# A Strassen step in the first product of a mixture-of-experts layer, with token groups outermost, and a second buffer for z_prev

## The chip, the cores and the metric

The kernel runs on one core of one Trainium2 chip. The metric is the device time of one execution in microseconds (us). The engines have short names in what follows: PE is TensorE (PEld its weight loads), DVE is VectorE, ACT is ScalarE, POOL is GpSimd, and SP is the engine whose queue issues most DMA transfers. PE's results go to tiles in PSUM; the other tiles of the chip's own memory lie in SBUF.

## The reference, cut to what matters

```python
# attention with a memory, B=4, H=8, S=576, D=64
local   = softmax(causal(q @ k.T / sqrt(D))) @ v
q_p     = where(q > 0, q, exp(q) - 1) + 1
mem_out = (q_p @ M_prev) / (q_p . z_prev + 1e-6)
x       = sigmoid(beta) * mem_out + (1 - sigmoid(beta)) * local      # reshaped to [2304, 512]

# mixture of experts, N=2304 tokens, D=512, E=8 experts, F=1024
P = exp(x @ w_gate - max)
repeat 8 times:                      # Sinkhorn
    P /= P.sum(1) + 1e-9;  P /= P.sum(0) + 1e-9;  P *= N / E
out = sum over e of  P[:, e] * (max(x @ w1[e], 0) @ w2[e])
```

All inputs and the output are float32.

## The kernel before

The kernel has two stages that overlap a little. `attention()` works through 16 pairs of heads in a software pipeline. For each pair, `load` issues some twenty DMAs on SP's queue, among them three for `z_prev` into one tile `zb` (lines 227 to 236). `phi_` multiplies the feature map by `zb` on POOL (lines 270 and 274), `r_trans` sends a small table through DRAM and back on SP's queue (lines 447 to 456), and `comb` multiplies, splits and stores the result as two tiles `xh` and `xl` (lines 503 to 507). A value x is kept as a high part in the type float32r and a low part x - high; a product of two such values is three matmuls, high*high, high*low and low*high. In attention the order of PE's work is written out by hand (`tc.manual_schedule`, line 531); on the other engines, and for all engines in the experts, the Tile framework orders the instructions by the program's order and its own cost estimates, and puts in the semaphore waits.

`experts()` computes h = relu(x @ w1) and y = h @ w2. F is cut into quarters of 256 columns, so that there are 32 quarters over 8 experts. A quarter's first product (`layer1`, line 617) makes 2 row blocks of 128 for each chunk of tokens; a chunk is 512 tokens, four times, and 256 tokens, once. Each row block and chunk takes 4 blocks of the inner dimension times 3 passes, 12 matmuls. ACT takes relu out of PSUM into the high part (line 622) and DVE makes the low part from PSUM and the high part (line 623). The second product (`layer2`, line 636) makes a tile of 128 tokens by 512 columns with 6 matmuls per quarter, and DVE adds it to `acc`, scaled by the router's P (line 685). `acc` holds all 18 tiles of 128 tokens.

The order is weights outermost: a unit of work is a pair of quarters (`UNITS`, line 601), and within it all five chunks. So each quarter's weights are loaded once; `w_task` loads 256 KB on SP's queue into a ring of two buffers (`wst`) and POOL splits them (lines 117 and 118) while another unit is computed. Quarter 0 alone is computed for chunks 0 to 2 already inside attention, into a DRAM tile `ydr`, and read back into `acc` later (line 696). The router's eight Sinkhorn rounds (`rows` and `colsum`, lines 571 to 593) are strewn between the first units; each has eight small DVE instructions and one sum over partitions on PE (line 581). PSUM has six buffers for all of this (`ps_s`), plus one each with the tags x and f.

Of the kernel before, what the change touches and what calls it, by code (L numbers as in the profile page):

```python
# [17 lines left out]
def kernel(  # L18
# [13 lines left out]
    nc = tc.nc  # L32
# [24 lines left out]

    def w_slot(pool, nm):
        return {
            key: pool.tile([128, KD, FQ] if key[1] == "1" else [128, FQ // 128, DM], F32R,  # L60
                           name=f"{key}{nm}")
            for key in ("w1h", "w1l", "w2h", "w2l")
        }
# [5 lines left out]
    hq = [h_tiles(static, "0")]  # L69

    ident = const.tile([128, 128], F32, name="ident")
    hmask = const.tile([128, 2], F32, name="hmask")
    ident2 = const.tile([128, 64], F32, name="ident2")
    ones = const.tile([128, 128], F32, name="ones")
    mask = const.tile([128, 640], F32, name="mask")
    mask4 = const.tile([128, 288], F32, name="mask4")
    gcol = const.tile([128, HP, 9], F32, name="gcol")
    ogb = const.tile([128, HP, 2, 64], F32, name="ogb")
    gt = const.tile([128, 2, H], F32, name="gt")
# [5 lines left out]
    mx = const.tile([128, 2], F32, name="mx")  # L85

# [9 lines left out]
    def w_task(qu, j):  # L96
        e, part = divmod(qu, NQ)
        dst = slots[qu % len(slots)] if len(slots) > 1 else slots[0]
        raw = wst_p.tile([128, 512], F32, tag="wst", name="wst")
        if j < 2:  # L100
            nc.sync.dma_start(
                out=raw.rearrange("p (k f) -> p k f", k=2),
                in_=w1[e, 256 * j:256 * j + 256, part * FQ:part * FQ + FQ]
                .rearrange("(k p) f -> p k f", p=128),
            )
            hi, lo = (dst[a][:, 2 * j:2 * j + 2].rearrange("p k f -> p (k f)")
                      for a in ("w1h", "w1l"))
        else:
            r0 = part * FQ + (j - 2) * 128
            nc.sync.dma_start(out=raw, in_=w2[e, r0:r0 + 128, :])  # L110
            hi, lo = dst["w2h"][:, j - 2], dst["w2l"][:, j - 2]

        def split():
            if qu == 1:
                nc.scalar.copy(out=hi, in_=raw)  # L115
            else:
                nc.gpsimd.tensor_copy(out=hi, in_=raw)  # L117
            nc.gpsimd.tensor_tensor(out=lo, in0=raw, in1=f32(hi), op=ALU.subtract)  # L118

        return split  # L120


    def setup():
        make_identity(nc, ident)
        nc.vector.tensor_tensor(
            out=ident2, in0=ident[:, 0:64], in1=ident[:, 64:128], op=ALU.add
        )
        nc.vector.memset(ones, 1.0)
        nc.vector.memset(hmask, 0.0)
        for h in range(2):  # L130
            nc.vector.memset(hmask[64 * h:64 * h + 64, h:h + 1], 1.0)
# [49 lines left out]
    def attention():  # L181
        with ExitStack() as actx:
# [8 lines left out]
            zb = ap1.tile([128, 2, 128], F32, name="zb")  # L191
# [11 lines left out]
            for t_ in (*mraw, zb, qn4, e4t):  # L203
                nc.vector.memset(t_, 0.0)
# [4 lines left out]
            def load(p):  # L209
                b, hp = divmod(p, HP)  # L210
                for src, dst in ((q, qraw[p % 2]), (k, kraw[p % 2]), (v, vraw[p % 2])):
# [16 lines left out]
                    out=zb[:, 0, :],  # L228
# [3 lines left out]
                for h in range(2):  # L232
                    nc.sync.dma_start(
                        out=zb[half[h], 1, half[h]],
# [26 lines left out]
            def phi_(p):  # L261
                tmp = ap1.tile([128, 5, 128], F32, tag="tmp", name="tmp", bufs=1)
                phi = ap1.tile([128, 5, 128], F32, tag="phi", name="phi", bufs=2)
                st[p]["phi"], st[p]["tmp"] = phi, tmp
                nc.scalar.activation(out=tmp, in_=qraw[p % 2], func=AF.Exp)
# [256 lines left out]
            for j in range(4):  # L522
                seq.append((0.5 + 0.5 * j, lambda j=j: w_task(0, j)()))
# [77 lines left out]
    UNITS = [(0,), (1,)] + [(qu, qu + 1) for qu in range(2, E * NQ, 2)]  # L601
    NU = len(UNITS)
    LAST0 = NQ // 2

    def h_of(u, c, qu):
        return hq[(c if len(UNITS[u]) == 1 else qu) % len(hq)]

    def layer1(u, c, m, ps_new):
        c0, cn = CHUNKS[c]
        qu = UNITS[u][m // 2]  # L610
        ws, (hh, hl) = slots[qu % len(slots)], h_of(u, c, qu)
        f = m % 2
        pt = ps_new()
        n = 0
        for kt in range(KD):
            for wt, x in ((ws["w1h"], xh), (ws["w1h"], xl), (ws["w1l"], xh)):
                nc.tensor.matmul(  # L617
                    out=pt[:, 0:cn], lhsT=wt[:, kt, 128 * f:128 * f + 128],
                    rhs=x[:, kt, c0:c0 + cn], start=(n == 0), stop=(n == 3 * KD - 1),
                )  # L620
                n += 1
        nc.scalar.activation(out=hh[:, f, 0:cn], in_=pt[:, 0:cn], func=AF.Relu)  # L622
        nc.vector.scalar_tensor_tensor(  # L623
            out=hl[:, f, 0:cn], in0=pt[:, 0:cn], scalar=0.0, in1=f32(hh[:, f, 0:cn]),
            op0=ALU.max, op1=ALU.subtract,
        )

    def layer2(u, c, j, ps_new):
        pt = ps_new()
        cols = slice(128 * j, 128 * j + 128)  # L630
        n, last = 0, 6 * len(UNITS[u]) - 1
        for qu in UNITS[u]:
            ws, (hh, hl) = slots[qu % len(slots)], h_of(u, c, qu)
            for f in range(2):
                for h_, wt in ((hh, "w2h"), (hh, "w2l"), (hl, "w2h")):
                    nc.tensor.matmul(  # L636
                        out=pt, lhsT=h_[:, f, cols], rhs=ws[wt][:, f],
                        start=(n == 0), stop=(n == last),
                    )
                    n += 1  # L640
        return pt

# [4 lines left out]
    ydr = dram.tile([NEARLY * 4, 128, DM], F32, name="ydr")  # L647

    def early_parts():
# [3 lines left out]
        def l2(c, j):  # L653
            pt = layer2(0, c, j, ps_f)
            yst = wst_p.tile([128, DM], F32, tag="wst", name="wst")
            nc.vector.tensor_copy(out=yst, in_=pt)
            nc.sync.dma_start(out=ydr[4 * c + j], in_=yst)

        parts = []
        for c in range(NEARLY):  # L660
            parts.append(
                [lambda c=c, m=m: layer1(0, c, m, ps_f) for m in range(2)]
                + [lambda c=c, j=j: l2(c, j) for j in range(4)]
            )
        return parts

    def experts():
        mp = ctx.enter_context(tc.tile_pool(name="mp", bufs=1, reuse_waits="tile"))
        slots.extend(w_slot(mp, str(j)) for j in (1, 2, 3))
        hq.append(h_tiles(mp, "1"))  # L670
        acc = mp.tile([128, NTILE, DM], F32, name="acc")

# [3 lines left out]
        def part2(u, c, j):  # L676
            pt = layer2(u, c, j, ps_t)
            e = UNITS[u][0] // NQ
            t_ = CHUNKS[c][0] // 128 + j
            if u == 0:  # L680
                nc.vector.tensor_copy(out=acc[:, t_], in_=pt)
            elif e == 0:
                nc.vector.tensor_tensor(out=acc[:, t_], in0=pt, in1=acc[:, t_], op=ALU.add)  # L683
            else:
                nc.vector.scalar_tensor_tensor(  # L685
                    out=acc[:, t_], in0=pt, scalar=P[:, t_, e:e + 1], in1=acc[:, t_],
                    op0=ALU.mult, op1=ALU.add,
                )
            if u == NU - 1:
                eng = nc.sync if t_ % 2 == 0 else nc.scalar  # L690
                eng.dma_start(out=out[128 * t_:128 * t_ + 128, :], in_=acc[:, t_])

        for j in range(4):
            w_task(1, j)()
        for t_ in range(4 * NEARLY):
            nc.sync.dma_start(out=acc[:, t_], in_=ydr[t_])
        for u in range(NU):
# [59 lines left out]
```

## Time and profile before

| what | value |
|---|---|
| median of 3 runs | 1880.23 us (1879.83 to 1882.64) |
| the profiled execution | 1881.86 us, span in its profile 1880.1 us |
| granted TensorE clock, mean | 0.985 |
| PE / PEld busy | 96% / 80% of the span |
| DVE / ACT / POOL busy | 35% / 20% / 20% of the span |
| DMA | 67.12 MB, mean 36 GB/s |

A view of groups gives one line for all instructions of one source line, engine, operation and shape: how many, their busy time in us, the mean duration of one in ns, and the idle time of the engine just before them with what ended it. Matmuls are pipelined and the profile models their ends, so that the rows of matmuls in a stream overlap; what one costs in a stream is the distance from its start to the next one's start. A view of stretches gives each engine's busy time and number of instructions in a stretch of the span. The chain of waits is followed back from the last instruction, at each step to what released it; a piece of the chain with a count, over several instructions in a row, is the time that these took together.

### The profile page before, as it was taken

To read this page: it belongs to the slowest core of one execution; us is meant where nothing else is said; L and a number is where in the kernel's file an instruction comes from. 1 tells how busy PE (TensorE), PEld (TensorE's weight loads), DVE (VectorE), ACT (ScalarE), POOL (GpSimd) and SP (SyncE) were. 2 spreads that over 40 slices of the span, in tenths; PEclk is the share of its full clock that TensorE was granted. 3 is DMA by queue.
4 is the path that set the end of the run, shared out by engine and by line. 5 is a ranking of instruction groups with operands and counts; after the bars stand their busy time and mean duration, and the time that the engine had idled before them with its cause. 6 is when DMAs were issued, how large, how long until landed. Compare 5 with 4: busy or idle time off the path is not lost.

```text
span 1880.1 us, 22876 instructions
## 1 busy us (share of the span) xinstructions
PE 1808.5 (96%) x9147; PEld 1496.3 (80%) x9147; DVE 660.4 (35%) x1423; ACT 367.0 (20%) x877; POOL 369.4 (20%) x423
## 2 busy tenths in 40 slices
PE   5788888899999999999999999999999999999999
PEld 4566676788888888888888888888888888888887
DVE  6767674733322222222222222222222222222222
ACT  4666565011111111011111111111111111111110
POOL 4544444410303020111202030303030303030000
PEclk8989899999999999999999999999999999999999
DMA  4333323200101010000101010101010101010011
GB/s 105 97 80 87 84 53 126 82 23 1 46 0 40 6 30 16 21 25 12 34 6 40 1 46 1 45 1 45 0 46 1 46 0 46 1 34 1 1 45 56
DMA packets 101546, 67.12 MB, mean 36 GB/s; under 512 B 67264, under 2 KB 85824, under 8 KB 101440
## 3 DMA queue, kind: packets, MB, share of 16 engines
q1 hardware_dynamic: 100144, 63.30, 11.9%
q10 hardware_dynamic: 1296, 2.36, 0.3%
q8 instruction: 72, 1.18, 0.3%
q14 instruction: 34, 0.28, 0.0%
HBM read 57.69 MB, written 7.94 MB: 35 GB/s over the span
## 4 chain that ended last, share of the span: by engine, by line
PE 86%; DMA 3%; DVE 3%; POOL 3%; ACT 2%; issue 2%; SPq 1%; ACTq 0%; POOLq 0%; DVEq 0%
PE s L617 41%; PE s L636 40%; ACT e L333 1%; DMA wst<-in_moe_w_dram 1%; DMA rsb<-rd 1%; PE x L479 1%; PE s L370 1%; DVE e L326 1%; PE f L636 1%; PE s L312 1%; POOL xc L503 1%; ACT e L356 1%; DMA zb<-in_z_prev_dram 1%; POOL tmp L270 0%; POOL phi L434 0%
## 5 line engine op out<-in xcount | busy, mean ns | idle before, releaser
L617 PE MATMUL s<-xh,w1h 128*128 128x512 f32 (+1 forms) x1256 | 463.0, 369 | 0.0
L617 PE MATMUL s<-xl,w1h 128*128 128x512 f32 (+1 forms) x1256 | 462.4, 368 | 0.0
L617 PE MATMUL s<-xh,w1l 128*128 128x512 f32 (+1 forms) x1256 | 462.3, 368 | 0.0
L622 ACT ACTIVATE hh<-s 128x512 fp32r<-128x512 f32 (+1 forms) x314 | 174.0, 554 | 1366.8 <-PE s L617 1327.8
L636 PE MATMUL s<-w2h,hh 128*128 128x512 f32 x1128 | 439.7, 390 | 0.0
L636 PE MATMUL s<-w2h,hl 128*128 128x512 f32 x1128 | 438.8, 389 | 0.4 <-DVE hl L623 0.4
L636 PE MATMUL s<-w2l,hh 128*128 128x512 f32 x1128 | 438.8, 389 | 0.0
L623 DVE SCALAR_TENSOR_TENSOR hl<-s,hh 128x512 fp32r<-128x512 f32 (+1 forms) x314 | 199.9, 637 | 600.9 <-ACT hh L622 600.8
L685 DVE SCALAR_TENSOR_TENSOR acc<-s,P,acc 128x512 f32<-128x512 f32 x252 | 189.2, 751 | 463.2 <-PE s L636 463.2
L617 PEld LDWEIGHTS s<-xl,w1h 128*128 128x128 f32 x1256 | 237.4, 189 | 39.7
L617 PEld LDWEIGHTS s<-xh,w1h 128*128 128x128 f32 x1256 | 237.3, 189 | 39.6
L617 PEld LDWEIGHTS s<-xh,w1l 128*128 128x128 f32 x1256 | 237.3, 189 | 39.3
L117 POOL CAST w1h<-wst 128x512 fp32r<-128x512 f32 x62 | 38.0, 612 | 1073.5 <-PE s L617 1055.8
L636 PEld LDWEIGHTS s<-w2h,hl 128*128 128x128 f32 x1128 | 211.6, 188 | 45.5 <-DVE hl L623 1.6
L636 PEld LDWEIGHTS s<-w2h,hh 128*128 128x128 f32 x1128 | 211.8, 188 | 44.1 <-ACT hh L622 1.0
L636 PEld LDWEIGHTS s<-w2l,hh 128*128 128x128 f32 x1128 | 211.8, 188 | 42.9
L118 POOL TENSOR_TENSOR w2l<-wst,w2h 128x512 fp32r<-128x512 f32 x64 | 82.4, 1289 | 8.1 <-ACT w2h L115 3.1
L118 POOL TENSOR_TENSOR w1l<-wst,w1h 128x512 fp32r<-128x512 f32 x64 | 82.9, 1295 | 5.3 <-ACT w1h L115 0.5
L333 ACT ACTIVATE e<-e,mn 128x512 f32<-128x512 f32 (+3 forms) x128 | 70.3, 550 | 21.0 <-DVE mn L326 21.0
L326 DVE CUSTOM_DVE_ANT_0 e<-s,mask 128x512 f32<-128x512 f32 (+3 forms) x128 | 55.1, 484 | 9.0 <-PE s L312 9.0
L117 POOL CAST w2h<-wst 128x512 fp32r<-128x512 f32 x62 | 37.9, 611 | 58.1 <-PE s L636 42.1
L683 DVE TENSOR_TENSOR acc<-s,acc 128x512 f32<-128x512 f32 x36 | 24.9, 691 | 33.0 <-PE s L636 32.9
(169 smaller groups left out, 1129.2 us busy)
## 6 DMA issues: line engine op xcount, KB each, us to landing
wst<-in_moe_w_dram SPq DMA_DIRECT2D x128, 256.0 KB
rsb<-rd SPq DMA_DIRECT2D x32, 144.0 KB
qraw<-in_q_dram SPq DMA_DIRECT2D x32, 128.0 KB
kraw<-in_k_dram SPq DMA_DIRECT2D x32, 128.0 KB
vraw<-in_v_dram SPq DMA_DIRECT2D x32, 128.0 KB
ydr<-wst SPq DMA_DIRECT2D x12, 256.0 KB
acc<-ydr SPq DMA_DIRECT2D x12, 256.0 KB
out_dram<-acc SPq DMA_DIRECT2D x9, 256.0 KB
```

Source lines behind the costliest of these rows:

```text
L117: nc.gpsimd.tensor_copy(out=hi, in_=raw)
L118: nc.gpsimd.tensor_tensor(out=lo, in0=raw, in1=f32(hi), op=ALU.subtract)
L312: nc.tensor.matmul(out=sp[h][:, at:at + w], lhsT=qq[x][half[h], 128 * i:128 * i + 128], rhs=kk[y][half[h], 0:w], start=(a == 0), stop=(a = ...
L326: nc.vector.tensor_tensor_reduce(out=et[:, h, 0:w], in0=sp[h][:, at:at + w], in1=mask[:, c0:c0 + w], scale=-SCALE, scalar=3.0e38, op0=ALU. ...
L333: nc.scalar.activation(out=et[:, h, 0:w], in_=et[:, h, 0:w], func=AF.Exp, scale=-1.0, bias=mn[:, c:c + 1], accum_out=sm_[:, c:c + 1],)
L356: nc.scalar.activation(out=e4[:, 0:576], in_=e4[:, 0:576], func=AF.Exp, scale=-1.0, bias=mn[:, 8:9], accum_out=sm_[:, 8:9],)
L617: nc.tensor.matmul(out=pt[:, 0:cn], lhsT=wt[:, kt, 128 * f:128 * f + 128], rhs=x[:, kt, c0:c0 + cn], start=(n == 0), stop=(n == 3 * KD - 1),)
L622: nc.scalar.activation(out=hh[:, f, 0:cn], in_=pt[:, 0:cn], func=AF.Relu)
L623: nc.vector.scalar_tensor_tensor(out=hl[:, f, 0:cn], in0=pt[:, 0:cn], scalar=0.0, in1=f32(hh[:, f, 0:cn]), op0=ALU.max, op1=ALU.subtract,)
L636: nc.tensor.matmul(out=pt, lhsT=h_[:, f, cols], rhs=ws[wt][:, f], start=(n == 0), stop=(n == last),)
L683: nc.vector.tensor_tensor(out=acc[:, t_], in0=pt, in1=acc[:, t_], op=ALU.add)
L685: nc.vector.scalar_tensor_tensor(out=acc[:, t_], in0=pt, scalar=P[:, t_, e:e + 1], in1=acc[:, t_], op0=ALU.mult, op1=ALU.add,)
```

## The change

The first product is done in seven half-size products in place of eight. Tokens are cut into three groups of 768 (`NG`, two halves of `HT` = 384 tokens), the inner dimension into two halves of 256, and the quarter into its two row blocks of 128. With weights A (blocks a11, a21, a12, a22) and tokens B, the weights' combinations are made for every item by POOL, with ACT taking their high parts (`w1_split`); the four combinations of tokens are made once per group (`t_tasks`). Seven products of 6 matmuls of 384 tokens each go to three PSUM buffers (`prod`); ACT copies the first, DVE adds the others up in SBUF tiles X, U2 and U3 (`temps`), and the four results are taken through relu and split from SBUF (`relu_split`). The second product (`second`) is as before, on items of one quarter each, so 6 matmuls to a PSUM tile and one DVE addition to `acc`.

The order is now groups outermost: for each group, all quarters but the first, which is done for all tokens beforehand through `ydr`. So there are 93 items, and each item loads and splits its weights anew. The first two items and the two before each change of group use the plain product (`plain`): 4 results of 12 matmuls of 384 tokens. In an item, the products of item q are interleaved with the six tiles of the second product of item q-1, and pieces of the weights' split (`jobs`), of the router (`tick`) and of the next group's combinations (`todo`) are strewn between them. `acc` holds one group, is written out with the group's last item, and read again from `ydr`.

In attention, `zb` becomes two tiles in turn. The tiles used only by attention, and those used only by quarter 0, move to pools that are closed after use; two tiles that nothing reads are dropped.

```diff
-            zb = ap1.tile([128, 2, 128], F32, name="zb")
+            zb2 = [ap1.tile([128, 2, 128], F32, name=f"zb{j}") for j in range(2)]
...
-        mp = ctx.enter_context(tc.tile_pool(name="mp", bufs=1, reuse_waits="tile"))
-        slots.extend(w_slot(mp, str(j)) for j in (1, 2, 3))
...
+    HT = 384
+    NG = NT // (2 * HT)
...
+        ITEMS = [
+            (g, e, part) for g in range(NG) for e in range(E) for part in range(NQ)
+            if (e, part) != (0, 0)
+        ]
+        per = E * NQ - 1
+        plain = {0, 1} | {g * per - j for g in range(1, NG) for j in (1, 2)}
...
+        def t_tasks(g):
+            th, tl = tcomb
+            s0, s1, s2 = (temps[:, i] for i in range(3))
+            d, p_ = nc.vector, nc.gpsimd
...
+            def split(i, src, eng):
+                nc.scalar.copy(out=th[:, i], in_=src)
+                sub(tl[:, i], src, f32(th[:, i]), eng)
+
+            return [
+                lambda: full(s0, 0, 1, d), lambda: full(s1, 0, 0, d), lambda: full(s2, 1, 1, p_),
+                lambda: sub(s1, s0, s1, d), lambda: split(0, s1, p_), lambda: sub(s0, s2, s0, d),
+                lambda: split(2, s0, p_), lambda: sub(s2, s2, s1, d), lambda: full(s0, 1, 0, d),
+                lambda: split(1, s2, p_), lambda: sub(s0, s0, s2, d), lambda: split(3, s0, d),
+            ]
...
+            raws = [mp.tile([128, 512], F32, tag="raw", name="raw", bufs=2) for _ in range(2)]
...
+            def comb_a():
+                tt(out=a22, in0=a21, in1=a22, op=ALU.add)
+                tt(out=a21, in0=a11, in1=a21, op=ALU.subtract)
+
+            def comb_b():
+                tt(out=a11, in0=a22, in1=a11, op=ALU.subtract)
+                tt(out=a12, in0=a12, in1=a11, op=ALU.subtract)
+
+            if q in plain:
+                return [lambda: two(1, r1), lambda: one(0, a11), lambda: one(3, a21)]
+            return [
+                lambda: two(1, r1), lambda: one(0, a11), comb_a, comb_b,
+                lambda: two(3, r0), lambda: two(5, r1),
+            ]
...
+        def relu_split(q, f, th, src):
+            hh, hl = hs[q % 2]
+            c = slice(HT * th, HT * th + HT)
+            nc.scalar.activation(out=hh[:, f, c], in_=src, func=AF.Relu)
+            nc.vector.scalar_tensor_tensor(
+                out=hl[:, f, c], in0=src, scalar=0.0, in1=f32(hh[:, f, c]),
+                op0=ALU.max, op1=ALU.subtract,
+            )
+
+        def prod(q, ops):
+            pt = pp[count[0] % 3]
+            count[0] += 1
+            wh, wl = w1s[q % 2]
+            n, total = 0, 6 * len(ops)
+            for wi, (xh_, xl_) in ops:
+                for k in range(2):
+                    for w, x in ((wh, xh_), (wh, xl_), (wl, xh_)):
+                        nc.tensor.matmul(
+                            out=pt[:, 0:HT], lhsT=w[:, wi, k], rhs=x[:, k],
+                            start=(n == 0), stop=(n == total - 1),
+                        )
+                        n += 1
+            return pt[:, 0:HT]
...
+            def p1():
+                nc.scalar.copy(out=X, in_=prod(q, [(0, b11)]))
+            def p6():
+                add(U2, prod(q, [(3, t2)]), X)
+            def p2():
+                add(X, prod(q, [(1, b21)]), X)
+                relu_split(q, 0, 0, X)
+            def p7():
+                add(U3, prod(q, [(4, t3)]), U2)
+            def p4():
+                add(X, prod(q, [(2, t4)]), U3)
+                relu_split(q, 1, 0, X)
+            def p5():
+                pt = prod(q, [(6, t1)])
+                add(U2, pt, U2)
+                add(U3, pt, U3)
+                relu_split(q, 1, 1, U3)
+            def p3():
+                add(U2, prod(q, [(5, b22)]), U2)
+                relu_split(q, 0, 1, U2)
+            return [[p1, p6, p2], [p7, p4], [p5, p3]]
...
+        jobs = w1_split(0, w1_load(0))
+        acc_load(0)
+        for c in range(NEARLY, len(CHUNKS)):
+            for f in first_parts(c, ps_s):
+                f()
+                if c == NEARLY:
+                    tick()
+                if jobs:
+                    jobs.pop(0)()
...
+        for q in range(NI + 1):
+            jobs = []
+            if q < NI:
+                jobs += w2_split(q, r2.pop(q))
+            if q + 1 < NI:
+                jobs += w1_split(q + 1, w1_load(q + 1))
+                jobs.insert(2, lambda q=q: r2.__setitem__(q + 1, w2_load(q + 1)))
+            if q in plain and q + 1 in plain and q:
+                todo += t_tasks(q // per + 1)
+            groups = (first_plain if q in plain else first_fast)(q) if q < NI else [[], [], []]
+            for i, grp in enumerate(groups):
...
+                if q:
+                    for j in (2 * i, 2 * i + 1):
+                        second(q - 1, j)
...
+            if q < NI and q and q % per == 0:
+                acc_load(q // per)
```

More of the change, by code (lines that the diff above doesn't have):

```diff
@@ L108, in w_task @@
         else:
-            r0 = part * FQ + (j - 2) * 128
-            nc.sync.dma_start(out=raw, in_=w2[e, r0:r0 + 128, :])
+            r0 = (j - 2) * 128
+            nc.sync.dma_start(out=raw, in_=w2[0, r0:r0 + 128, :])
             hi, lo = dst["w2h"][:, j - 2], dst["w2l"][:, j - 2]
[L113 to L120, printed above, removed]
+        nc.gpsimd.tensor_copy(out=hi, in_=raw)
+        nc.gpsimd.tensor_tensor(out=lo, in0=raw, in1=f32(hi), op=ALU.subtract)
     def setup():
         make_identity(nc, ident)
-        nc.vector.tensor_tensor(
-            out=ident2, in0=ident[:, 0:64], in1=ident[:, 64:128], op=ALU.add
-        )
         nc.vector.memset(ones, 1.0)
-        nc.vector.memset(hmask, 0.0)
-        for h in range(2):
-            nc.vector.memset(hmask[64 * h:64 * h + 64, h:h + 1], 1.0)
         nc.gpsimd.memset(mask, 0.0)
@@ new lines, in w1_split, with one, two @@
+        def w1_split(q, raws):
+            wh, wl = w1s[q % 2]
+            r0, r1 = (r.rearrange("p (k f c) -> p k f c", k=2, f=2) for r in raws)
+            a11, a21, a12, a22 = r0[:, :, 0], r0[:, :, 1], r1[:, :, 0], r1[:, :, 1]
+            tt = nc.gpsimd.tensor_tensor
+            def one(i, src):
+                nc.scalar.copy(out=wh[:, i], in_=src)
+                tt(out=wl[:, i], in0=src, in1=f32(wh[:, i]), op=ALU.subtract)
+            def two(i, raw):
+                src = raw.rearrange("p k f c -> p f k c")
+                nc.scalar.copy(out=wh[:, i:i + 2], in_=src)
+                tt(out=wl[:, i:i + 2], in0=src, in1=f32(wh[:, i:i + 2]), op=ALU.subtract)
+            def comb_a():
[9 more added lines that the diff above has]
+                lambda: two(3, r0), lambda: two(5, r1),
+            ]
@@ new lines, in w2_split, with one @@
+        def w2_split(q, raws):
+            wh, wl = w2s[(q + 1) % 2]
+            def one(j):
+                nc.scalar.copy(out=wh[:, j], in_=raws[j])
+                nc.gpsimd.tensor_tensor(
+                    out=wl[:, j], in0=raws[j], in1=f32(wh[:, j]), op=ALU.subtract
+                )
+            return [lambda: one(0), lambda: one(1)]
+        def relu_split(q, f, th, src):
[5 more added lines that the diff above has]
+                op0=ALU.max, op1=ALU.subtract,
+            )
@@ new lines, in second, with acc_load @@
+            if q % per == per - 1:
+                eng = nc.scalar if g == NG - 1 and j % 2 else nc.sync
+                eng.dma_start(out=out[128 * t_:128 * t_ + 128, :], in_=acc[:, j])
+        def acc_load(g):
+            for j in range(2 * HT // 128):
+                nc.sync.dma_start(out=acc[:, j], in_=ydr[2 * HT // 128 * g + j])
+        NI = len(ITEMS)
+        jobs = w1_split(0, w1_load(0))
[7 more added lines that the diff above has]
+                    jobs.pop(0)()
```

245 lines of the change are left out of this document (142 added, 103 removed).

## The prediction

> **What bounds the kernel now.** I read the page first, then the stretches, then the end of the chain of waits.
>
> ```profile
> span 1880.1 us, 22876 instructions
> PE 1808.5 (96%) x9147; PEld 1496.3 (80%) x9147; DVE 660.4 (35%) x1423; ACT 367.0 (20%) x877; POOL 369.4 (20%) x423
> ...
> PEclk8989899999999999999999999999999999999999
> ```
>
> In the stretches the columns after the length are each engine's busy time (number of instructions), the granted clock, the DMA share and GB/s.
>
> ```profile
> 300.00:350.00 50.00, 40.33 (x220) 30.97 (x218) 20.92 (x62) 13.63 (x35) 25.08 (x29) 0.93 0.46 143
> 900.00:1100.00 200.00, 200.00 (x929) 167.59 (x928) 53.58 (x78) 22.81 (x41) 32.65 (x36) 1.00 0.08 24
> ```
>
> From about 360 us on PE is never idle and runs at the full clock, as in the second stretch; DVE, ACT and POOL are busy 27%, 11% and 16% of it. The experts' time is therefore the number of matmuls times the distance between their starts. The end of the chain gives that distance, since its pieces are runs of matmuls with nothing between them (start, length, what):
>
> ```profile
> 1843.15 10.88 PE s L617 x48
> 1854.03 10.88 PE s L636 x48
> 1864.91 5.75 PE s L617 x48
> ...
> 1876.17 0.75 DVE acc L685
> ```
>
> A matmul with 512 tokens costs 10.88/48 = 0.2267 us in both products; one with 256 tokens (the short chunk) 5.75/48 = 0.1198. So an instruction costs nearly what its width says, and the weight load of each one hides at least down to 0.12 us.
>
> **First product: the gain.** No expert matmul is 384 wide. A line through the two widths gives 0.1198 + (0.2267 - 0.1198)/2 = 0.1733 us; strict proportion to 512 gives 0.170. I take 0.1733, as it lies on both rows. The first quarter stays; 31 are left.
> - Before, a quarter takes 4 chunks x 24 x 0.2267 + 24 x 0.1198 = 24.64 us; 31 take 763.8.
> - After, 87 fast items take 7 x 6 = 42 matmuls, 7.28 us each, 633.2; 6 plain items take 48, 8.32 us each, 49.9; together 683.1.
> - Gain 80.7 us (93.8 at 0.170).
>
> The second product keeps its count: 93 items x 6 tiles x 6 = 3348, as 31 quarters x 18 tiles x 6. An item's share is 36 x 0.2267 = 8.16 us, so a fast item has a **PE period of 15.44 us**.
>
> The Trainium skill, "TensorE: Matmul & The Clock Gate", section "Back-to-back issue gap", puts an isolated warm matmul at N/2.4 + 2.5 ns. That would be 0.216 us at 512 and 0.1625 at 384; the trace has 0.2267 at 512, so the rule is too low here; by it alone the fast items would save another 87 x 42 x 0.0108 = 39 us.
>
> **What must fit behind those 15.44 us.** The new work runs on engines that were idle, so I cost it by the nearest shapes.
>
> ```profile
> L685 DVE SCALAR_TENSOR_TENSOR acc<-s,P,acc 128x512 f32<-128x512 f32 x252 | 189.2, 751 | 463.2 <-PE s L636 463.2
> L623 DVE SCALAR_TENSOR_TENSOR hl<-s,hh 128x512 fp32r<-128x512 f32 x250 | 172.8, 691 | 537.0 <-ACT hh L622 536.9
> L623 DVE SCALAR_TENSOR_TENSOR hl<-s,hh 128x256 fp32r<-128x256 f32 x64 | 27.0, 423 | 63.9 <-ACT hh L622 63.9
> L267 DVE SCALAR_TENSOR_TENSOR phi<-qraw,tmp 128x640 f32<-128x640 f32 x16 | 14.0, 874 | 0.4 <-issue 0.2
> L622 ACT ACTIVATE hh<-s 128x512 fp32r<-128x512 f32 x250 | 149.5, 598 | 1131.7 <-PE s L617 1092.6 <-DMA out_dram<-acc 39.1
> L622 ACT ACTIVATE hh<-s 128x256 fp32r<-128x256 f32 x64 | 24.5, 383 | 235.1 <-PE s L617 235.1
> L118 POOL TENSOR_TENSOR w1l<-wst,w1h 128x512 fp32r<-128x512 f32 x64 | 82.9, 1295 | 5.3 <-ACT w1h L115 0.5
> L507 POOL TENSOR_TENSOR xl<-xc,xh 128x256 fp32r<-128x256 f32 x16 | 11.7, 732 | 1.3 <-ACT xh L506 1.3
> ```
>
> - DVE, per fast item: 7 additions out of PSUM at 384, half way between 691 and 423 = 0.557, 3.9 us; 6 additions to acc at 0.751, 4.5; 4 low parts from SBUF, 0.55 (874 x 384/640, 0.52, and a little for the fixed part), 2.2. Sum 10.6. Each low part first waits for ACT's relu, about 0.49 (between 598 and 383): up to 2.0 more, if nothing fills it.
> - ACT: a copy and 4 relus at 0.49, 2.5; weights' high parts, five at 0.6 and one at 0.38, 3.4. Sum 5.9.
> - POOL: w2, 2 x 1.29; w1, 3 x 1.29 + 5 x 0.73 (four combinations, one low part). Sum 10.1.
>
> All below 15.44, so covered. What is queued behind what: ACT's high parts stand in its queue behind the relus, and these behind PE's products; DVE's acc additions stand behind low parts that wait for ACT. Three buffers for products and three for tiles give PE some 3 us before a late addition stops it: p6 reuses the buffer of p5, read by 13.0 us of the item, at 15.44 + 1.04.
>
> A second bound is DVE's waiting for POOL. Rows in order of time (start, length):
>
> ```profile
> 343.14 1.27 POOL L118 TENSOR_TENSOR w1l<-wst,w1h 128x512 fp32r<-128x512 f32 x1
> ...
> 343.63 0.94 DVE L575 TENSOR_TENSOR Pt<-P,rs 128x144 f32<-128x144 f32 x1
> ...
> 363.82 0.31 DVE L575 TENSOR_TENSOR Pt<-P,rs 128x144 f32<-128x144 f32 x1
> ```
>
> The same DVE instruction, both inputs in SBUF, takes 0.31 alone and 0.94 when it starts inside a POOL instruction: it ends 0.16 us after POOL's. The low parts out of PSUM do not show it (mean 691 beside a POOL 16% busy). In the new item the 4 low parts have both inputs in SBUF, and POOL is busy 10.1 of 15.44 us, so each waits between 0 and 1.29 us; I take 65% x half of 1.1 = 0.36, 1.4 per item. DVE then needs 10.6 + 1.4 + 2.0 = 14.0 of 15.44 us.
>
> The Trainium skill, "SBUF — State Buffer", section "Who interferes with whom", says the same as a rule: a DVE instruction with two SBUF inputs contends with a GpSimd instruction that reads SBUF, and whichever is second blocks fully. This rule speaks against the change; the trace agrees (0.94 against 0.31).
>
> **The weights' cycle.** Raw w1 has two buffers and an item needs both, so the next load starts when POOL has finished this item's split.
>
> ```profile
> 337.72 2.66 DMA wst<-in_moe_w_dram
> ```
>
> A load lands 2.66 us after the wait before it ends. Then ACT 0.6, POOL 7.5, one more wait for ACT 0.6: 11.4 us, and 13 with hand-offs and with POOL blocked by DVE (up to 4 x 0.55). The 2.6 us for w2 fit into the load's wait. Below 15.44, so covered, and the last two combinations are needed only at p5, 10.6 us into the next item. For small stalls in a fast item I take 0.1 us (bounds 0 and 0.3), +8.7 for 87.
>
> **Start of the experts.** PE's stalls there now (the bracket is the idle time before):
>
> ```profile
> 325.30 0.61 PE L550 MATMUL s<-ident,ls 16*128 16x16 f32 x4 [5.08 <-ACT ls L546]
> ...
> 326.43 0.63 PE L617 MATMUL s<-xl,w1h 128*128 128x512 f32 x1
> 326.86 0.63 PE L617 MATMUL s<-xh,w1l 128*128 128x512 f32 x1
> ...
> 355.61 0.48 PE L581 MATMUL cp<-Pt,ones 128*128 128x144 f32 x2 [1.95 <-DVE Pt L575]
> ```
>
> The 5.08 us wait for a buffer of the ring that the weight loads share; w1's raw tiles now have their own. Matmuls after it start 0.43 apart, twice the usual, 12 of them: 2.4 us more. Up to 12 us can go, with the router's waits. New is DVE's load in items 0 and 1: seven of eight router rounds (2.2 us each, from the round below less its wait), 8 combinations of 768 columns (874 x 768/640 = 1.05 each), 8 low parts at 0.557 and 6 additions at 0.69: 15.4 + 8.4 + 4.5 + 4.1 = 32 us, before waits for POOL, against PE's 2 x 8.32 + 8.16 = 24.8.
>
> ```profile
> 362.99 0.29 DVE L572 TENSOR_REDUCE rs<-P 128x18 f32<-128x144 f32 x1
> ...
> 364.80 0.31 DVE L585 TENSOR_REDUCE cs<-cp 128x8 f32<-128x144 f32 x1 [0.67 <-PE cp L581]
> ...
> 365.59 0.31 DVE L590 SCALAR_TENSOR_TENSOR P<-Pt,cs 128x144 f32<-128x144 f32 x1
> ```
>
> So PE idles 7 us there, or 18 with waits for POOL; less what goes, -5 to +11. I take +3 (bounds -12 and +11).
>
> **Changes of group, attention, tail.** SP issues nine loads of acc in a row now:
>
> ```profile
> 320.67 4.31 SPq L696 DMA_DIRECT2D acc<-ydr  x9
> ```
>
> At each change it has 6 stores and 6 such loads to issue (0.48 us each); the last acc load waits for the last store, 2.66 or so, and the next weights' load stands behind it, about 5 us late. The cycle has 2.4 us of slack per item, and the late combinations are needed late: +2 each, two of them (bounds 0 and 10 each), +4. The next combinations of tokens, 12 tasks, fall into two plain items, where DVE has only 4 x 0.557 + 4.5 = 6.7 of 16.5 us to do, so nothing; without that cover they cost DVE's 8 us. In attention, SP waits for POOL to free zb:
>
> ```profile
> SPq L227 <- POOL tmp L270: 2.9, 3, 1.5
> SPq L227 <- POOL tmp L274: 1.9, 5, 0.5
> ```
>
> That is 4.8 us in 8 waits, with the r table's load queued behind some; the two waits go, the load of the first pair doesn't move. What is late next is that table. I take -2 (bounds -5 and +2, as the order on SP is made anew). Dropped and moved tiles: nothing, they stand ahead of the first loads. The last item's six stores come 1.36 us apart instead of 2.72: +1 (0 to 2).
>
> **Sum.** -80.7 + 8.7 + 3 + 4 - 2 + 1 = -66.0. From the profiled execution, 1881.9 (span 1880.1), that is 1815.9; it lies 1.6 above the median of the runs, 1880.23, so I forecast **1814 us**. Its own range, from the bounds: 1797 to 1842.
>
> **Rivals.**
> - *DVE becomes the bound, through its waits for POOL (slower).* If the four waits are 1.0 us each, DVE needs 10.6 + 2.0 + 4.0 = 16.6 us per fast item, 1.2 over PE: 87 x 1.2 = 104, less the 8.7 counted, 1909. It decides from a period of 15.44 + (66 + 8.7)/87 = 16.3 us on. For it: the 0.94 row. Against: POOL isn't always busy, and acc additions can fill the waits for relu.
> - *The weights' cycle or ACT's queue sets the period, partly.* 13 us with 2.4 us of slack; if ACT's high parts come 3 us late behind relus, the period is about 16.0: 87 x 0.56 - 8.7 = +40, 1854. For it: one load's buffers in effect; against: late weights are needed late.
> - *The narrow matmul is cheaper or the start clean.* 0.170 and no new stall at the start: 1814 - 13 - 8 = 1793. For it: the 120 ns row may be the weight load's own pace, so that the line is too steep.
> - *The Strassen step brings nothing*, since with 384 tokens the weight load is no longer hidden. Were it 0.19 us per matmul, the fast items would give 87 x 42 x 0.017 = 62 back: 1876. Against: 0.1198 at 256.
>
> **How the numbers follow.** Forecast 0.66, DVE 0.11, weights 0.14, cheaper 0.06, weight load 0.03. The range that holds 8 in 10 leaves out the DVE case, the weight load and the far side of the others: 1793 to 1860. A difference under 0.2% (4 us) can't be told from no change. Faster: the forecast, the weights' case and the cheaper one, 0.86. Slower: the DVE case and a third of the weight load's, 0.12. Same: the rest of that, 0.02.
>
> **What would show it.** Right: 384-wide matmuls 0.173 us apart; PE busy near 100% from item 2 on at the full clock; a fast item each 15.4 to 15.6 us; DVE about 70% busy. DVE wrong: low parts over 1 us, PE idle before p6 or p1 released by DVE. Weights wrong: PE idle released by POOL or ACT's w1 tiles, once per item. Start: idle before L581's successor, released by DVE, in 7 to 18 us. The prediction falls if matmuls are 0.19 apart or if PE idles over 0.8 us per item.

## The result, and the profile after

| | before | after |
|---|---|---|
| median of 4 runs each, us | 1880.03 (1876.44 to 1882.64) | 1827.12 (1825.03 to 1828.61) |
| ratio to before, 95% interval | | 0.972 (0.970 to 0.974) |
| span of the profiled execution, us | 1880.1 | 1825.7 |

The kernel became 52.9 us faster. The forecast was 1814, so a fifth of the expected 66 us is missing. The first lines of the page of the changed kernel:

```profile
span 1825.7 us, 27237 instructions
PE 1748.1 (96%) x9369; PEld 1538.5 (84%) x9369; DVE 1329.2 (73%) x2385; ACT 729.0 (40%) x1586; POOL 1139.8 (62%) x1091
...
PEclk8999999899999999999999999999999999999999
```

PE is still busy 96% of the span, and DVE now 73%, POOL 62%. The stretches, with the columns as before (length, then each engine's busy time and count, clock, DMA share, GB/s):

```profile
700.00:900.00 200.00, 196.86 (x975) 177.01 (x974) 143.57 (x207) 71.97 (x138) 132.91 (x120) 0.99 0.25 80
900.00:1100.00 200.00, 200.00 (x1001) 180.58 (x1000) 150.68 (x223) 72.75 (x139) 137.85 (x128) 1.00 0.22 69
```

Inside a group PE has no gap, as before: 200.00 of 200. The first of these stretches holds a change of group, and there 3.14 us are missing. The end of the chain of waits shows a whole fast item and the tail (start, length, what):

```profile
1782.60 3.14 PE s L788 x18
1785.74 2.76 PE s L620 x12
1788.51 2.10 PE s L788 x12
1790.61 2.76 PE s L620 x12
1793.37 2.10 PE s L788 x12
1795.48 2.76 PE s L620 x12
1798.24 3.14 PE s L788 x18
...
1811.12 10.94 PE s L620 x48
...
1822.08 0.75 DVE acc L863
```

An item takes 1798.24 - 1782.60 = 15.64 us. The prediction had 15.44 of matmuls. Twelve 384-wide ones take 2.10 instead of 12 x 0.1733 = 2.08, and twelve 512-wide ones 2.76 instead of 12 x 0.2267 = 2.72, although nothing is between them.

The distances from each matmul's start to the next one's, over the whole of both traces, give an account that adds up to the difference of the spans. "Idle" is a distance over 0.6 us longer than the width's own, "slow" one longer by 0.06 to 0.6.

| term, us | forecast | before | after | difference |
|---|---|---|---|---|
| matmuls at 0.2267, 0.1733 and 0.1198 us | -80.7 | 1543.6 | 1463.0 | -80.6 |
| extra in the first nine matmuls after a change of width | +8.7 as "small stalls" | 0.5 | 18.3 | +17.8 |
| idle and slow, start of the experts | +3 | 16.1 | 18.8 | +2.7 |
| idle and slow, changes of group | +4 | 0 | 10.6 | +10.6 |
| start of attention's last matmul | -2 | 312.0 | 307.7 | -4.4 |
| from the last matmul's start to the end | +1 | 4.3 | 4.1 | -0.3 |
| other matmuls, rest | 0 | | | -0.2 |
| sum | -66.0 | | | -54.4 |

Two terms carry the miss: the change of width and the changes of group.

**The changes of group.** PE at the first of the two (start, length, instruction, in brackets the idle time before it and what ended it):

```profile
808.26 0.40 PE L620 MATMUL s<-w2h,hhl 128*128 128x512 f32 x1
811.80 0.58 PE L620 MATMUL s<-w2h,hhh 128*128 128x512 f32 x1 [3.14 <-DVE acc L863]
812.18 0.63 PE L620 MATMUL s<-w2l,hhh 128*128 128x512 f32 x1
812.60 0.63 PE L620 MATMUL s<-w2h,hhl 128*128 128x512 f32 x1
```

PE waits for a tile of PSUM, that is for DVE's addition to `acc`. After the stop the matmuls start 0.42 to 0.43 apart, half the usual speed, until 815.3. The second change is the same (3.19 us). DVE and POOL in that time:

```profile
800.11 0.74 DVE L863 SCALAR_TENSOR_TENSOR acc<-s,P,acc 128x512 f32<-128x512 f32 x1
800.77 3.38 DVE L694 TENSOR_TENSOR temps<-temps 128x768 f32<-128x768 f32 x2
804.07 0.55 DVE L773 SCALAR_TENSOR_TENSOR hhl<-s,hhh 128x384 fp32r<-128x384 f32 x1
804.54 2.15 DVE L694 TENSOR_TENSOR temps<-temps 128x768 f32<-128x768 f32 x1
806.61 0.55 DVE L773 SCALAR_TENSOR_TENSOR hhl<-s,hhh 128x384 fp32r<-128x384 f32 x1
808.45 2.54 DVE L688 TENSOR_TENSOR temps<-xh,xl 128x768 f32<-128x768 f32 x1 [1.29 <-POOL tl L694]
810.91 0.74 DVE L863 SCALAR_TENSOR_TENSOR acc<-s,P,acc 128x512 f32<-128x512 f32 x1
811.57 0.94 DVE L694 TENSOR_TENSOR temps<-temps 128x768 f32<-128x768 f32 x1
```

```profile
799.32 4.01 POOL L762 TENSOR_TENSOR w2l<-raw,w2h 128x512 fp32r<-128x512 f32 x2
803.29 6.88 POOL L694 TENSOR_TENSOR tl<-temps,th 128x768 fp32r<-128x768 f32 x3
```

Between two additions to `acc`, at 800.11 and 810.91, stand four combinations of the next group's tokens. One that starts while POOL is idle takes 0.94 (at 811.57); these take 1.7 to 2.5, all beside a POOL that is busy without a gap until 810.17, and the last one also waits 1.29 until POOL has read the scratch tile that it overwrites. DVE takes its instructions one after another, in the order of these rows, so the addition that PE needs stands behind them.

**The start.** PE's long stops there:

```profile
349.36 0.69 PE L788 MATMUL s<-xh,w1h 128*128 128x384 f32 x1 [4.49 <-DVE hhl L773]
354.01 0.82 PE L572 MATMUL cp<-Pt,ones 128*128 128x144 f32 x2 [3.97 <-DVE Pt L566]
```

The 5.08 us of before are gone, and three shorter stops follow these two; the five together take 11.4 us, all released by DVE. DVE just before the first of them:

```profile
343.00 1.26 DVE L579 TENSOR_SCALAR cs<-cs 128x8 f32<-128x8 f32 x1
...
346.06 1.46 DVE L688 TENSOR_TENSOR temps<-xh,xl 128x768 f32<-128x768 f32 x1 [1.56 <-POOL tl L694]
347.44 1.39 DVE L581 SCALAR_TENSOR_TENSOR P<-Pt,cs 128x144 f32<-128x144 f32 x1
348.75 0.55 DVE L773 SCALAR_TENSOR_TENSOR hhl<-s,hhh 128x384 fp32r<-128x384 f32 x1
```

A router's instruction on 8 numbers a partition takes 1.26 us here; its P instruction took 0.31 in the row of before that the prediction shows (0.556 on average there) and takes 1.39. The low part that PE waits for stands behind both kinds of work.

**The new shapes on POOL and DVE**, in the page's groups (instruction and count, busy time, mean ns of one, idle time before and what ended it):

```profile
L739 POOL TENSOR_TENSOR w1l<-raw,w1h 128x512 fp32r<-128x512 f32 x267 | 368.5, 1394 | 392.9 <-ACT w1h L738 392.9
L821 DVE TENSOR_TENSOR temps<-s,temps 128x384 f32<-128x384 f32 x609 | 330.2, 555 | 128.3 <-PE s L788 83.4
L863 DVE SCALAR_TENSOR_TENSOR acc<-s,P,acc 128x512 f32<-128x512 f32 x504 | 361.2, 741 | 38.2 <-PE s L620 37.7
```

The additions take 0.555 and 0.741 us, where the prediction put 0.557 and 0.751. The low parts, in the view of groups of DVE alone, first from SBUF in the fast items, then out of PSUM in the plain ones:

```profile
L773 DVE SCALAR_TENSOR_TENSOR hhl<-temps,hhh 128x384 fp32r<-128x384 f32 x348 | 322.7, 946 | 184.9 <-ACT hhh L772 184.5
...
L773 DVE SCALAR_TENSOR_TENSOR hhl<-s,hhh 128x384 fp32r<-128x384 f32 x24 | 13.3, 553 | 19.8 <-ACT hhh L772 19.7
```

### The profile page after: what moved, and what is told of

Its sections match the earlier page's. It is cut to its first block, busy times and chain, and to the rows that moved or that the text cites. A ratio compares the mean times of both kernels' runs of the same rounds, so it can differ in the third digit from the quotient of the medians.

```text
span 1825.7 us, 27237 instructions
## 1 busy us (share of the span) xinstructions
PE 1748.1 (96%) x9369; PEld 1538.5 (84%) x9369; DVE 1329.2 (73%) x2385; ACT 729.0 (40%) x1586; POOL 1139.8 (62%) x1091
## 4 chain that ended last, share of the span: by engine, by line
PE 82%; POOL 5%; DVE 3%; issue 3%; ACT 3%; DMA 2%; SPq 1%; POOLq 0%; ACTq 0%; DVEq 0%
PE s L620 41%; PE s L788 35%; PE x L470 1%; ACT e L324 1%; DMA rsb<-rd 1%; PE s L303 1%; POOL tl L694 1%; POOL w2l L762 1%; POOL xc L494 1%; PE s L361 1%; ACT e L347 1%; POOL w1l L739 0%; PE x L475 0%; PE f L620 0%; POOL phi L425 0%
## 5 line engine op out<-in xcount | busy, mean ns | idle before, releaser
L739 POOL TENSOR_TENSOR w1l<-raw,w1h 128x512 fp32r<-128x512 f32 x267 | 368.5, 1394 | 392.9 <-ACT w1h L738 392.9
L773 DVE SCALAR_TENSOR_TENSOR hhl<-temps,hhh 128x384 fp32r<-128x384 f32 x348 | 322.7, 946 | 184.9 <-ACT hhh L772 184.5
L620 PE MATMUL s<-w2h,hhh 128*128 128x512 f32 x1116 | 435.3, 390 | 6.5 <-DVE acc L863 6.3
L620 PE MATMUL s<-w2h,hhl 128*128 128x512 f32 x1116 | 440.7, 395 | 0.0
L620 PE MATMUL s<-w2l,hhh 128*128 128x512 f32 x1116 | 440.2, 394 | 0.0
L821 DVE TENSOR_TENSOR temps<-s,temps 128x384 f32<-128x384 f32 x609 | 330.2, 555 | 128.3 <-PE s L788 83.4
L762 POOL TENSOR_TENSOR w2l<-raw,w2h 128x512 fp32r<-128x512 f32 x186 | 270.3, 1472 | 26.5 <-ACT w2h L761 26.5
L788 PE MATMUL s<-th,w1l 128*128 128x384 f32 x696 | 234.9, 337 | 0.0
L788 PE MATMUL s<-th,w1h 128*128 128x384 f32 x696 | 234.4, 337 | 0.0
L788 PE MATMUL s<-tl,w1h 128*128 128x384 f32 x696 | 233.8, 336 | 0.0
```

Of the source, the lines that this page charges most:

```text
L620: nc.tensor.matmul(out=pt, lhsT=h_[:, f, cols], rhs=w[:, f], start=(n == 0), stop=(n == 5))
L739: tt(out=wl[:, i:i + 2], in0=src, in1=f32(wh[:, i:i + 2]), op=ALU.subtract)
L762: nc.gpsimd.tensor_tensor(out=wl[:, j], in0=raws[j], in1=f32(wh[:, j]), op=ALU.subtract)
L773: nc.vector.scalar_tensor_tensor(out=hl[:, f, c], in0=src, scalar=0.0, in1=f32(hh[:, f, c]), op0=ALU.max, op1=ALU.subtract,)
L788: nc.tensor.matmul(out=pt[:, 0:HT], lhsT=w[:, wi, k], rhs=x[:, k], start=(n == 0), stop=(n == total - 1),)
L821: nc.vector.tensor_tensor(out=o, in0=x, in1=y, op=ALU.add)
```

## The experiments

Ratios are to runs of the kernel before on the same chip.

### A second buffer for z_prev, alone and taken away

The first kernel is the one before with two `zb` tiles and nothing else, the second the changed one with a single tile.

```diff
# in the kernel before
-            zb = ap1.tile([128, 2, 128], F32, name="zb")
+            zb2 = [ap1.tile([128, 2, 128], F32, name=f"zb{j}") for j in range(2)]
# in the changed kernel
-            zb2 = [ap1.tile([128, 2, 128], F32, name=f"zb{j}") for j in range(2)]
+            zb2 = [ap1.tile([128, 2, 128], F32, name=f"zb{j}") for j in range(1)]
```

> The kernel before with two z_prev tiles alone. In the profile of the changed kernel attention's last matmul starts 4.4 us earlier than before (307.65 against 312.03 us). Theory: the second tile does that, so this run ends 3 to 5 us below before (about 1876). Rival: the earlier end comes from the other moves (pools, dropped tiles, another order on the queues), so this run is within 1.5 us of before.

> The changed kernel with one z_prev tile. Theory that the second tile gives 4 us: 1831, with attention's last matmul back at about 312 us. Rival, that it gives nothing: 1827 and 307.7.

Alone, the second tile gives 1873.91 us (ratio 0.9968, 0.9956 to 0.9981). Taking it away gives 1831.36 (0.9739, 0.9725 to 0.9752; with it 0.9719, 0.9700 to 0.9738). These intervals touch, and the traces tell the two apart: attention's last matmul starts at 312.03 with one tile in both programs, at 308.32 and 307.65 with two. In all twelve traces of kernels with two tiles it lies between 304.1 and 308.4; so the second tile is worth some 4 us, and from one trace to the next this start moves by as much. The way is not the one described: in the changed kernel SP still waits 3.8 us for POOL, against 4.8 before and 5.3 in the changed kernel with one tile (time in all, number of waits, the longest).

```profile
SPq L217 <- POOL tmp L261: 2.1, 3, 0.9
SPq L217 <- POOL tmp L265: 1.7, 4, 0.6
```

Which transfer came earlier isn't settled.

### Fewer changes of matmul width

Theory: a change of width costs PE some 66 ns per pair (there and back), three pairs an item. Rival: the extra comes from traffic of other engines, and is there whatever the order. A second rival, that it is the change from one product to the other that costs, is answered by the trace of before: there PE changes products at 512 wide 120 times after 400 us, 60 each way, and the next nine distances add up to 0.3 ns less than their own. The two kernels keep every matmul and change the order within an item: 3 products, 3 tiles, 4 products, 3 tiles (two pairs), or 7 products, then 6 tiles (one pair).

```diff
-            return [[p1, p6, p2], [p7, p4], [p5, p3]]
+            return [[p1, p6, p2], [p7, p4, p5, p3]]
# or
+            return [[p1, p6, p2, p7, p4, p5, p3], [], []]
```

> Two blocks per item (three products, three tiles, four products, three tiles): four changes of width. Theory of the changes: period 0.066 us less, 6 us less in all (1821), with less waiting for buffers than with one block. Rival of the traffic: 1827.

> All seven products of an item first, then the six tiles of the second product: two changes of matmul width per item instead of six. Theory that each pair of changes (512 to 384 and back) costs 66 ns, as the distances after a change say: a period of 15.51 us where nothing else stops PE, 0.13 less than 15.64, so 11 to 12 us less in all (1815), unless the three product buffers make PE wait for DVE, which would show as idle time before p7 to p3. Rival, that the matmuls are slowed by the traffic of DVE, ACT and POOL, which is unchanged: period 15.6 and 1827.

The extra after a change of width fell from 18.3 us with three pairs to 12.2 with two and 6.2 with one: 93 items x 66 ns = 6.1 for each. The item with two blocks, in the chain of waits of that kernel:

```profile
1780.29 4.18 PE s L788 x24
1784.48 4.12 PE s L620 x18
1788.60 3.15 PE s L788 x18
1791.74 4.12 PE s L620 x18
1795.87 4.18 PE s L788 x24
```

That is 1795.87 - 1780.29 = 15.58. **Two blocks: 1816.09 us, ratio 0.9661 (0.9647 to 0.9676)**, faster than both kernels. By the account of its trace 6.1 us come from the width, and 7.8 from the changes of group, where idle and slow matmuls fall from 10.6 to 2.8; the start takes 3.0 more. Why the stops at the changes nearly go with this order was not tested.

One block is slower than the kernel before: 1976.7 us, ratio 1.051 (1.049 to 1.053). The group of PE's first tile matmuls, and an item on DVE and ACT:

```profile
L620 PE MATMUL s<-w2h,hhh 128*128 128x512 f32 x1116 | 446.8, 400 | 142.7 <-DVE acc L863 128.3 <-DVE acc L859 14.4
```

```profile
1000.17 2.11 DVE L773 SCALAR_TENSOR_TENSOR hhl<-temps,hhh 128x384 fp32r<-128x384 f32 x2 [2.18 <-ACT hhh L772]
1002.20 2.05 DVE L863 SCALAR_TENSOR_TENSOR acc<-s,P,acc 128x512 f32<-128x512 f32 x3
```

```profile
998.27 0.62 ACT L738 CAST w1h<-raw 128x512 fp32r<-128x512 f32 x1 [3.30 <-POOL raw L747]
...
999.62 0.94 ACT L772 ACTIVATE hhh<-temps 128x384 fp32r<-128x384 f32 x2
```

This is the second rival of the prediction, in another order of work: ACT holds the weights' high part and waits 3.30 us for POOL's combination, two relus stand behind it, DVE waits 2.18 for the relu, three additions to `acc` stand behind that, and PE stops 1.7 us in nearly every item. No engine is full (DVE is busy 65% of that span, PE 89%). The chain is read from the rows of one item; no run takes a link of it away.

### The same grouping without Strassen

All 93 items plain, 48 matmuls instead of 42, and no combinations.

```diff
-        plain = {0, 1} | {g * per - j for g in range(1, NG) for j in (1, 2)}
+        plain = set(range(len(ITEMS)))
```

> Groups outermost and all else as changed, but all 93 items with the plain product: no Strassen step, no combinations of tokens. Theory, that PE sets the time in both: 87 items gain 6 matmuls of 0.1733 us each, +90.5 us, less the stalls that the combinations of tokens make at the start and at the two changes of group (about 6 each at the changes, some 7 at the start, together 15 to 20), so 1898 to 1905: above before, the regrouping alone a loss. Rival, that part of the fast items' time is DVE's or POOL's: less than +70, below 1890.

1894.72 us, ratio 1.0077 (1.0055 to 1.0099): 0.8% slower than before. The matmuls by themselves take 9.8 us more, as 48 of 384 cost more than their share at 512, and the width changes 17.9; a cleaner start and attention give back 8.7 and 5.2. The extra after a change of width is the same 18.4 us, although DVE and POOL do much less, which refutes the rival of traffic in the section before:

```profile
900.00:1100.00 200.00, 200.00 (x1009) 181.74 (x1008) 82.75 (x127) 54.52 (x108) 64.31 (x60) 1.00 0.20 64
```

It came out between the two ranges expected, because leaving out the combinations clears more stops than the 15 to 20 us taken: idle and slow matmuls are 7.3 us in all, against 29.4 in the changed kernel. So Strassen's step itself takes away 90.5 us of matmuls (773.6 to 683.1), gives 22.1 back in stops, and nets 67.4 between the spans.

### The combinations at the changes of group

Two of the three groups are computed with the first group's combinations, so that DVE and POOL make none at the changes.

```diff
-            if q in plain and q + 1 in plain and q:
-                todo += t_tasks(q // per + 1)
```

> The combinations of tokens are made for the first group alone and used for all three, so two of three groups are computed from wrong combinations. Theory, that PE's stop of 3.2 us at each change of group and the slow matmuls after it come from DVE being held by these tasks: both stops go, 5.6 us each, 1816. Rival, that SP's stores and acc loads hold it up: stops stay, 1826.

1815.03 us, ratio 0.9652 (0.9628 to 0.9676). The stops are gone, and idle and slow matmuls there fall from 10.6 to 0.2 us. The stretch around the first change, in the changed kernel and in this one:

```profile
790.00:830.00 40.00, 36.86 (x178) 32.92 (x177) 28.40 (x35) 13.27 (x24) 25.40 (x18) 0.96 0.16 47
```

```profile
790.00:830.00 40.00, 40.00 (x202) 36.09 (x201) 19.32 (x30) 10.77 (x22) 16.13 (x16) 1.00 0.16 47
```

The stores and loads of `acc` on SP are still there, so they cost nothing.

### Three plain items in place of two

A third plain item at the start and at each change, and a task only at every second place.

```diff
-        plain = {0, 1} | {g * per - j for g in range(1, NG) for j in (1, 2)}
+        plain = {*range(3)} | {g * per - j for g in range(1, NG) for j in range(1, 3 + 1)}
...
+            if todo and slot[0] % 2 == 0:
+                todo.pop(0)()
```

> Three plain items at the start and at each change of group instead of two, and the tasks for the combinations of tokens in every second slot instead of every slot. Costs 3 items x 6 matmuls x 0.1733 = 3.1 us. Theory, that DVE's load in a short time makes the stops: 11 us of them go at the changes and some 5 at the start, 1814. Rival, that the stops come from the order alone and move along: 1830.

1828.76 us, 0.9725 (0.9704 to 0.9746): nothing gained. The stops at the changes are 3.19 and 3.21 us. DVE's order around them is that of the changed kernel: the framework orders instructions by their dependences and its own estimates, and gathers the tasks again. The stops stay, as the rival said, and a place in the program is no place on the engine. What a real spreading of the tasks on DVE would bring, this run does not show.

### A lighter POOL

From the fifth item on POOL leaves out the low parts of w1, so that the products use stale ones.

```diff
+            low = tt if q < 4 else lambda **_: None
-                tt(out=wl[:, i], in0=src, in1=f32(wh[:, i]), op=ALU.subtract)
+                low(out=wl[:, i], in0=src, in1=f32(wh[:, i]), op=ALU.subtract)
```

> From the fifth item on, POOL doesn't make the low parts of w1 (5 of its 9 us for w1 and w2 per item stay); old ones are used. Theory, that DVE's waits for POOL lie wholly behind PE: low parts on DVE fall from 0.95 toward 0.6 us and the time stays at 1827 (within 3 us). Rival, that POOL's traffic or DVE's waits slow the matmuls: 10 us or more less.

1824.33 us, 0.9703 (0.9679 to 0.9726), as the theory said. DVE's low parts in this kernel:

```profile
L774 DVE SCALAR_TENSOR_TENSOR hhl<-temps,hhh 128x384 fp32r<-128x384 f32 x348 | 190.3, 566 | 137.4 <-ACT hhh L773 136.8
```

They fall from 946 to 566 ns with POOL's busy time at half, and the extra after a change of width stays at 18.3 us. So the waits for POOL are real, 0.38 us less in each, and hidden behind PE inside a group.

### The start: which load is too much?

Four kernels, all on the order with two blocks. The first makes the first group's combinations earlier, beside the first quarter's last chunks, with `acc` as scratch, which is then loaded after them; the second also takes the Strassen step for the first two items.

```diff
+        todo = t_tasks(0)
         for c in range(NEARLY, len(CHUNKS)):
             for f in first_parts(c, ps_s):
...
+                if todo:
+                    todo.pop(0)()
# and in the second
-        plain = {0, 1} | {g * per - j for g in range(1, NG) for j in (1, 2)}
+        plain = {g * per - j for g in range(1, NG) for j in (1, 2)}
```

> Two blocks per item as in the run with two blocks, and the first group's combinations of tokens made earlier, strewn over quarter 0's last two chunks, where POOL is idle for 9.5 us, with acc as their scratch space (acc is loaded after them). Theory, that the stops at the start (4.5 and 4.0 us and 11 matmuls at half speed after them, 3 us) come from DVE and POOL doing these tasks and the router's rounds and holding each other up: most of them go, 8 to 10 us less than two blocks alone, 1807. Rival, that the router's rounds alone hold PE: 2 us less, 1814.

> The same with the first two items fast instead of plain, which PE does in 2.1 us less. Theory, that DVE, with seven router rounds (15 us) beside two fast items (12 us each), sets the time there: no gain or some us more than the run before. Rival, that DVE's work fits: 2 us less.

1819.29 us (0.9677, 0.9651 to 0.9702) and 1831.15 (0.9736, 0.971 to 0.9761), against 1816.09; the first can't be told from it, as the intervals overlap. The longest stops come earlier and end at 325 and 331 us, against 350, and idle time is 18.5 and 30.1 us over the whole span against 16.9: the theory that the combinations only had to be made earlier fell.

The last two each take away one of the loads that meet there: seven of the router's eight rounds, or the combinations (eight plain copies on ACT instead).

```diff
-        for _ in range(8):
+        for _ in range(1):
             tasks += [rows, colsum]
# or, for the first group
+                return [lambda i=i, t=t, x=x: cp3(t, x, i) for i in range(4) for t, x in ((th, xh), (tl, xl))]
```

> The version with two blocks of products per item, with one of the router's eight rounds; the other seven are left out, so P differs. It asks what holds PE at the start of the experts, where the version with two blocks has stops of 4.51, 3.95, 0.64, 2.35 and 0.60 us, four of them before the router's sum over partitions. Theory: the router's rounds are the load that DVE cannot get done in time (7 rounds of 2.2 us, 15.4 us of DVE); without them the four stops go, 7.5 us, and the first shrinks: 1806 us (1803 to 1810) against 1816. Rival: the combinations of tokens, with POOL, hold DVE; the stops move from the router's sum to the next matmul that needs DVE: 1813 or more.

> The version with two blocks of products per item, in which the first group's combinations of tokens are replaced by eight plain copies on ACT, so that the fast items of the first group compute from wrong combinations; DVE and POOL are free of them, the router's eight rounds stay. Theory (the router's rounds hold PE): the stop of 4.5 us shrinks, those before the router's sum stay: 1812 to 1816. Rival (the combinations hold DVE through POOL): the stops of 4.51 and 3.95 go with the half-clock matmuls behind them, 1806 (1803 to 1809). If both runs gain about as much, either load alone fits and only the two together do not.

1805.28 us (0.9591, 0.9569 to 0.9613) and 1807.94 (0.9605, 0.9588 to 0.9622). The stretch from 320 to 400 us with two blocks, then with one round, then with copies:

```profile
320.00:400.00 80.00, 67.35 (x330) 59.01 (x330) 60.98 (x119) 24.64 (x48) 47.92 (x40) 0.91 0.25 81
```

```profile
320.00:400.00 80.00, 73.53 (x360) 64.87 (x359) 47.05 (x78) 27.24 (x54) 53.29 (x47) 0.96 0.25 80
```

```profile
320.00:400.00 80.00, 73.90 (x376) 65.22 (x375) 55.13 (x125) 24.10 (x49) 41.68 (x42) 0.98 0.26 85
```

PE gains 6.2 and 6.6 us of work in this stretch. Idle time at the start falls from 16.2 us to 9.0 and 8.5; the kernel before had 10.9. (The router's rounds left out also take 1.7 us of small matmuls with them.) The longest stop that stays, with one round and then with copies:

```profile
346.94 0.69 PE L788 MATMUL s<-xh,w1h 128*128 128x384 f32 x1 [3.43 <-DVE hhl L773]
```

```profile
356.79 0.48 PE L572 MATMUL cp<-Pt,ones 128*128 128x144 f32 x2 [3.09 <-DVE Pt L566]
```

Neither theory of a single load holds: removing either load saves about the same, and each alone still stops PE. With one round, PE waits 3.43 us for a low part that stands behind the combinations on DVE, one of which waits 2.97 us for POOL; another stop of 2.23 us comes after them, in the first fast item. With copies, three stops before the router's sum stay, 0.88, 3.09 and 1.08 us. So both loads hold PE here, and that either alone would fit is not borne out.

## Why the prediction was right, and where not

- **The gain** was right: 384-wide matmuls are 0.1733 us apart, as the line through two widths said, and their sum is -80.6 against -80.7. The 0.1625 that follows from the rule of the Trainium skill, "TensorE: Matmul & The Clock Gate", section "Back-to-back issue gap", was not seen.
- **The 0.1 us of small stalls in a fast item was wrong in cause and short in size.** There are no stalls of hand-offs inside a group. The item is 0.20 us longer, 15.64 where 15.4 to 15.6 was named, because of three pairs of width changes: 17.8 us in place of 8.7. That this lies inside the bounds of 0 and 0.3 an item is luck, as they were set for something else. Two and one pairs, and the plain kernel, showed it. The trace of before had it too: after its 256-wide chunks the 512-wide matmuls take 27 ns more in sum. The prediction looked at pieces of 48 matmuls only, where this doesn't show.
- **"What must fit behind" was right:** low parts at 0.946 against 0.55 + 0.36 = 0.91 taken, DVE busy 150.68/200 = 75% of a stretch against (10.6 + 1.4)/15.44 = 78%. The first rival, DVE as the bound at 1909, didn't come.
- **The weights' cycle** did not show in the changed kernel. With one block its mechanism stops PE in nearly every item, at 1976.7 us: the slack lies in the order of products and tiles, not in the engines' loads.
- **The start, +3,** measured +2.7: the 5.08 went, and the new stops take 11.4 us, within the 7 to 18 named. The mechanism, DVE's load, was right; with bounds of -12 and +11, that the number is so close is in part luck.
- **The changes of group, +4 by SP's queue, and nothing for the combinations of tokens, because DVE had only 6.7 of 16.5 us to do, were wrong:** +10.6, all from the combinations, nothing from SP. The step that failed is to compare loads over two items. By the prediction's own estimate PE has some 3 us of buffers before a late addition to `acc` stops it, and four combinations nearly in a row, lengthened from 0.94 to as much as 2.5 us each beside POOL, take 8 us without counting the wait.
- **Attention and tail:** -4.4 and -0.3 against -2 and +1, both of small weight. That -4.4 lies in the bounds is luck: the waits from which it was worked out mostly stay.
- **"Its own range, from the bounds: 1797 to 1842"** does not follow by adding up: the bounds named for the terms give 1783 to 1861. The measured 1827 lies in both, and in the range of 8 in 10, 1793 to 1860.

The missing 11.6 us between the spans (66.0 - 54.4) are thus 9.1 from the width changes and 6.6 from the changes of group, less 2.4 in attention, 1.3 in the tail, 0.3 at the start and 0.2 in the rest, and 0.1 more in the matmuls.

## What to carry to other kernels

A fully busy engine does not run at one price per width: look at the first ten distances after each change of shape, and lay equal shapes together, until the buffers between the engines no longer cover the longer blocks. Cover is not a share of busy time: ask of each task strewn in how long it holds its engine, and whether the other side's buffers last that long. When two loads meet in one place, take each away alone before moving either.

## What the runs showed that was not expected

A change of width can cost even when both widths stream without a gap. Mean extra over the width's own distance, in ns, of the first, second and later matmuls after a change in the changed kernel, worked out from the starts:

```
512 to 384:  -2.4  1.7  4.1 11.6  2.5  8.3                    sum 26
384 to 512:   2.5  6.6  9.1 -2.5  4.1  9.1  1.6  5.8  4.1     sum 40
```

It is the same with DVE at 41% and at 75% of the stretch. Not every change costs: in the trace of before, 256 to 512 takes 27 ns more in sum and 512 to 256 takes 6 less. Why PE does this no run shows.

After a stop of 3.14 us the 512-wide matmuls start 0.43 us apart for some 3.5 us. The Trainium skill, "TensorE: Matmul & The Clock Gate", section "What's actually happening", says that an idle window of about 3.4 us halves the clock and as long a busy one restores it; the trace agrees in kind, with a stop that is a little shorter. In the kernel with the lighter POOL a stop of 2.78 us is followed by such a stretch too, and in the one-block kernel the stops of 1.7 us in nearly every item are not. Each stop at a change of group in the changed kernel costs 5.3 us (10.6/2), of which 3.1 to 3.2 is idle in the profile's brackets.

A DVE instruction with both inputs in SBUF takes 946 ns beside a POOL that is 69% busy, 566 beside one that is 37% busy (73.52 of 200), 553 when one input is in PSUM, in the plain items; POOL's own subtraction goes from 1295 to 1394.
